# A second token quarter of the query projection in seven-product form, and reciprocals broadcast by one transfer per half quarter, in a fused attention and token-mixing kernel

## Chip, cores and metric

The kernel runs on one core of one Trainium2 chip. The metric is the device time of one execution in microseconds (us). TensorE (PE) does the matrix products and loads its stationary operand as separate instructions (PEld); VectorE (DVE), ScalarE (ACT) and GpSimd (POOL) work beside it; SyncE (SP) issues nearly all transfers, which run on 16 DMA engines.

## What is computed

x has 2048 tokens (S) of 1024 numbers (D), in bf16. A linear-attention block with 32 heads of 32 is followed by an MLP that mixes tokens (F = 3584). The part that matters here is the attention:

```python
qkv = (layernorm(x) @ wqkv).reshape(B, S, 3, H, Dh).transpose(2, 0, 3, 1, 4)
q, k, v = qkv[0], qkv[1], qkv[2]
phi = lambda t: where(t > 0, t + 1, exp(t)) + 1e-6
pq, pk = phi(q), phi(k)
kv = einsum("bhsd,bhse->bhde", pk, v)
z = einsum("bhsd->bhd", pk)
num = einsum("bhqd,bhde->bhqe", pq, kv)
den = einsum("bhqd,bhd->bhq", pq, z)[..., None] + 1e-6
h = x + (num / den).transpose(0, 2, 1, 3).reshape(B, S, D) @ wo
```

Behind it stands `h + B(layernorm(h))` with `gelu(u @ w1 + b1) @ w2 + b2` over tokens; the change does not touch it.

## The kernel before, in words

**Tiling.** The token axis is cut into four quarters u = 0 to 3 of 512 tokens (`SW`, `NSC`), the features into eight blocks j of 128. `xnT` holds the normalised x transposed, `pqT` holds phi(q) transposed, [128, 8, 2048].

**Key and value steps.** `run_step` (L1119) writes out by hand the order of a pipeline of steps, `KRun` (keys) and `VRun` (values), each on 256 tokens with number q. A step is a Strassen-like scheme of seven products p1 to p7 in place of eight, each of four 128x512 matmuls (`Run.mm`, L973). It needs sums of token blocks (`x_sums`, L962, kept in `xs_sb`) and of weight blocks (`w_sums`, L947). `kv_accum` (L923) adds phi(k)ᵀv into `kv_ps`.

**The query projection in two forms.** One quarter, u = 2, is done in seven-product form by two steps of class `QRun` (one for each half of the features), between the steps of q = 5; a `QRun` product is eight matmuls of 256 columns (L1107). Its four weight sums are `tq`, two of which lie in `shared_sb`, two in the part of `pqT` of quarter 3. The other three quarters are done in plain form, in 24 units (u, j) of eight matmuls of 512 columns, listed in `q_units` (L1312). Units 0 to 7 (u = 0) are issued early by `q_fill` (L1302): three beside the first value step, and five around and behind the last value step. Units 8 to 23 (u = 1 and 3) come in a later loop, `for n, (u, j) in enumerate(q_units[8:])`, as `q_held`. Every unit ends in `phi_evac`: ACT makes an Exp and a Relu tile (L185, L187), DVE makes phi from them (L190, L194).

**What else the later loop does.** Tables say behind which n each of these follows. `fold` (four times) multiplies the kv blocks into wo (16 small matmuls, two copies on ACT, two on DVE). `den(u)` makes the denominators of a quarter (8 matmuls) and their reciprocals by Ln and Exp on ACT, and writes them, 128x512 fp16, to `rd_dram`. `den_spread(u)` reads them back so that each of the 32 rows of a head gets its head's reciprocal: for each half h of the features four transfers of 32 partitions x 4 x 512, 128 KB each, into one of three buffers (`thirds`). `scale_q(u, h)` multiplies that half of `pqT` by them on DVE. `first_sums` prepares the next stage on DVE (`sa`, `is`).

**The output stage.** `out_mm(i)` for 16 token tiles, 16 matmuls each (8 blocks j for each of two output halves), reads the scaled `pqT` of its quarter, in the order of `place(i)`; `seed(i)` copies x into its accumulators first (ACT), from rows that `load_xr` brought.

Accumulators come from `acc_tile`, which takes buffers of two pools in the order of `acc_ring`. What is marked `pin` or goes through `hv`, `ht`, `hs`, `hd` keeps the order in which it is written on its engine; the rest is put in place by the framework's scheduler. SP's transfers are issued in order: a transfer that waits holds up all behind it.

Of the kernel before, what the change touches and what calls it, by code (L numbers as in the profile page):

```python
# [21 lines left out]
DH = 32  # L22
# [8 lines left out]
def kernel(  # L31
# [13 lines left out]
    x = A_x.flatten_outer_dims()  # L45
# [3 lines left out]
    NS, ND, NF = S // P, D // P, F // P  # L49
# [5 lines left out]
    SW = min(BANK, S)  # L55
    NSC = S // SW
# [3 lines left out]
    QR = P // 4  # L60
# [8 lines left out]

    def more_acc(bufs):  # L70
        pool = accx.enter_context(tc.tile_pool(name="accx", bufs=bufs, space=PSUM))
        acc_ring[:] = [acc, pool, acc, pool, pool] if bufs == 3 else [pool, pool, pool, acc, acc, pool]

    def less_acc():
        accx.close()
# [703 lines left out]
    with ExitStack() as actx:  # L779
# [27 lines left out]
            return (q + b) % HB  # L807

        with ExitStack() as a1:
            a1w = a1.enter_context(tc.tile_pool(name="a1w", bufs=1))  # L810
            wkv = a1w.tile([P, ND, 2 * D], BF16)
            NVA, NPK = 4, 4
# [21 lines left out]
            e1pool = a1.enter_context(tc.tile_pool(name="e1pool", bufs=1))  # L834
            epool = a1.enter_context(tc.tile_pool(name="epool", bufs=2))
            xin = a1.enter_context(tc.tile_pool(name="xin", bufs=3))
            a1s = a1.enter_context(tc.tile_pool(name="a1s", bufs=4))
            trctx = ExitStack()
# [113 lines left out]
                v = xnT[:, :, q * 2 * P:(q + 1) * 2 * P].rearrange("p (k two) (h f) -> p k two h f", two=2, h=2)  # L952
                return v[:, :, 0, 0, :], v[:, :, 1, 0, :], v[:, :, 0, 1, :], v[:, :, 1, 1, :]

            def x_sums(q, part=slice(0, 4)):
                a11, a12, a21, a22 = x_blocks(q)
                sm = xs_sb[:, q % 2]
                for out, a, b, op in (
                    (sm[:, 0], a21, a22, ALU.add), (sm[:, 1], sm[:, 0], a11, ALU.subtract),
                    (sm[:, 2], a11, a21, ALU.subtract), (sm[:, 3], a12, sm[:, 1], ALU.subtract),  # L960
                )[part]:
                    pin(nc.vector.tensor_tensor(out, a, b, op))  # L962

# [124 lines left out]
            class QRun(KRun):  # L1088
                lean = True

                def __init__(self, u, half):
# [3 lines left out]
                    self.s1, self.s2, self.s3, self.s4 = (  # L1095
                        xs_sb[:, :, t].rearrange("p r k f -> p k r f") for t in range(4)
                    )
                    (self.b11, _, self.b21, self.b22), (self.t1, self.t2, self.t3, self.t4) = qmov

# [16 lines left out]
                def dst(self, h, c):  # L1116
                    n0 = self.u * SW + h * SW // 2
                    v = pqT[:, 4 * self.half:4 * self.half + 4, n0:n0 + SW // 2]
                    return v.rearrange("p (j two) n -> p j two n", two=2)[:, :, c, :]  # L1119

            def run_step(n, prev, after6=None, after5=None, after7=None, fill=None, after3=None):
                if n is not None:
# [186 lines left out]
                phi_evac(pqT[:, j, u * SW:(u + 1) * SW], qp[:, 0:SW], SW, a2k)  # L1309

            assert NSC == 4
            q_units = [(u, j) for u in (0, 1, NSC - 1) for j in range(ND)]  # L1312
            NVP = NS // 2
            q_next = iter(q_units)

            def q_fill():
                q_unit(*next(q_next))
# [20 lines left out]
            load_next(2 * G0)  # L1338
            prev = v1
            q_sums = {2: slice(0, 1), 3: slice(1, 2), 4: slice(2, 3), 5: slice(3, 4)}  # L1340
            for q in range(2, NVP):
                runs = [KRun(q), VRun(q)]
                if q == 5:
                    runs = [runs[0], QRun(q // 2, 0), runs[1], QRun(q // 2, 1)]
                for n in runs:
                    kind = type(n).__name__[0]
                    i = {"K": 2 * q + 3, "V": 2 * q + 4}.get(kind, NS)
                    if q == 5 and kind == "Q":
                        i = NS - 1 if n.half == 1 else NS
                    elif q == 6 and kind == "K":  # L1350
                        i = NS

                    def after6():
                        if i < NS:
                            ln_stats(i)

                    def after5():
                        if kind == "V":
                            kv_accum(2 * q - 2)
                            kv_accum(2 * q - 1)  # L1360
                        if i < NS:
# [24 lines left out]
            nc.vector.memset(zz[:, :, 3 * HB:], float(S))  # L1386
            turned = kvbd[:].rearrange("p (b a) (r e) -> p a b r e", b=HB, e=DH)
            sums_v = kv_ps[:, :, 0:DH].rearrange("p (b a) e -> p a b e", b=HB)
            for q in range(HB):
# [25 lines left out]
        pools["is_bufs"] = 4  # L1415
        a3p = actx.enter_context(ExitStack())
        ndp = a3p.enter_context(tc.tile_pool(name="ndp", bufs=2, space=PSUM))
        rd_dram = [dram.tile([P, SW], FP16, name=f"rd_dram{u}") for u in range(NSC)]

        with ExitStack() as a3:  # L1420

# [44 lines left out]
            def den_inv(u, ps):  # L1466
                hs.activation(ps[:], ps[:], ACT.Ln, bias=eps_den[:], scale=1.0 / S)
                hs.activation(rd_sb, ps[:], ACT.Exp, scale=-1.0)
                hd.dma_start(rd_dram[u][:], rd_sb)

            def den_spread(u):
                rows = rd_dram[u].rearrange("(g o h) n -> o h g n", g=4, h=HB)
                for h in range(2):
                    rdb = thirds[(2 * SPREAD.index(u) + h) % 3].bitcast(FP16).rearrange("p (j n) -> p j n", n=SW)
                    for q in range(HB):
                        hd.dma_start(
                            rdb[q * DH:(q + 1) * DH, :, :],
                            rows[h, q].unsqueeze(0).to_broadcast([DH, 4, SW]),
                        )
                    rdbs[u, h] = rdb  # L1480

            def den(u):
                den_inv(u, den_mm(u))
# [98 lines left out]
            for n, (u, j) in enumerate(q_units[8:]):  # L1582
                if n == len(q_units) - 8 - 1:
# [8 lines left out]
                if n == 3:  # L1592
                    for i in range(XRL + 1):
                        load_xr(i)
                if n in (12, 13):
                    load_w1(1, n % 2, pin)
# [259 lines left out]
```

## Time and profile before

| | |
|---|---|
| median of 3 runs | 555.93 us (555.36 to 556.04) |
| the profiled execution, its own time | 556.6 us |
| its span, first to last instruction | 554.8 us |
| TensorE busy, share of the span | 548.8 us, 99% |
| VectorE, ScalarE, GpSimd busy | 444.6, 289.0, 26.3 us |
| mean granted TensorE clock | 0.999 of full speed |
| bytes moved by the 16 DMA engines | 74.58 MB, mean 134 GB/s |

Times in the profile are counted from the first instruction of the span. The 1.8 us between the span and the profiled execution's own time lie around the span. A row of the timeline gives the start, the length, the engine, the line and the operation, its output and inputs, and in brackets how long the engine had been idle before it, and who ended that. The chain of waits is followed back from the last instruction; a piece names the engine, the output tile, the line and the number of instructions. Through the helpers `ht`, `hs`, `hv` and `hd` many operations share line 230.

The change lies between 107 us (the key step of q = 6) and 190 us (the first tiles of the output stage). In this stretch the list of waits names none of a matmul. VectorE is busy 6.68 us of the ten from 110, 5.53 of the ten from 120, 7.68 of the ten from 150, 9.38 of the ten from 160 and 7.34 of the ten from 170.

### The profile page before, as it was taken

The numbers are of one execution on the slowest core, as the hardware profiler recorded it, in microseconds if no ns is written. First come the engines' busy times: TensorE is split into PE (matmuls) and PEld (weight loads), VectorE is DVE, ScalarE is ACT, GpSimd is POOL, SyncE is SP. The second block draws the span as 40 slices with busy tenths as digits, with TensorE's granted clock in tenths as the row PEclk, the third lists the DMA queues.
The fourth block names the chain that finished last, engine by engine and source line by source line (L and its number), as shares of the span: only waits on it lengthen the run. The fifth ranks groups of instructions, "written<-read, shape, count | busy, mean of one in ns | idle before, by whom it ended". The sixth has DMA issues, their size and how long they took to land.

```text
span 554.8 us, 9799 instructions
## 1 busy us (share of the span) xinstructions
PE 548.8 (99%) x3801; PEld 316.3 (57%) x3819; DVE 444.6 (80%) x863; ACT 289.0 (52%) x614; POOL 26.3 (5%) x36
## 2 busy tenths in 40 slices
PE   9999999999999999999999999999999999999997
PEld 3444446644444444456666766666445667667665
DVE  6798888764597788889989789888986979749747
ACT  4747768675886877645546465564210412413310
POOL 1000000000000000000000000000002103103111
PEclk9999999999999999999999999999999999999999
DMA  8933331204677942103041340423868759849334
GB/s 296 311 77 77 77 78 39 40 1 141 207 205 224 314 167 78 71 1 123 30 152 29 125 152 2 152 48 86 220 219 207 201 138 241 211 143 219 91 108 74
DMA packets 83087, 74.58 MB, mean 134 GB/s; under 512 B 15826, under 2 KB 74464, under 8 KB 83040
## 3 DMA queue, kind: packets, MB, share of 16 engines
q1 hardware_dynamic: 78656, 69.87, 42.4%
q0 software_dynamic: 4096, 3.68, 4.9%
q8 instruction: 30, 0.49, 0.4%
q10 hardware_dynamic: 288, 0.39, 0.2%
q14 instruction: 17, 0.14, 0.1%
HBM read 59.12 MB, written 11.67 MB: 128 GB/s over the span
## 4 chain that ended last, share of the span: by engine, by line
PE 98%; issue 0%; ACT 0%; DVE 0%; DVEq 0%
PE psI L230 25%; PE psC L230 16%; PE acc_t L230 15%; PE psB L230 8%; PE psC L973 4%; PE psB L973 4%; PE psA L973 4%; PE acc_t L893 4%; PE acc_t L1302 2%; PE psB L342 2%; PE psA L342 2%; PE psE L973 2%; PE psC L342 2%; PE psA L230 1%; PE psE L342 1%; PE acc_t L97 1%
## 5 line engine op out<-in xcount | busy, mean ns | idle before, releaser
L230 PEld LDWEIGHTS <-is 128*128 128x128 f16 x736 | 71.8, 98 | 31.1 <-DVE hi L230 0.4
L230 PEld LDWEIGHTS <-sa 128*128 128x128 f16 x606 | 59.2, 98 | 27.1
L230 PEld LDWEIGHTS <-wq 128*128 128x128 bf16 (+1 forms) x496 | 48.5, 98 | 28.1 <-issue 1.0
L230 PE MATMUL acc_t<-wo_sb,pqT 128*128 128x512 f16 x256 | 55.6, 379 | 0.0
L487 POOL DMA_DIRECT2D out_dram<-wq x28 | 24.4, 935 | 516.5 <-DVE sa L334 397.5
L230 PEld LDWEIGHTS <-pqT 128*128 128x128 bf16 x256 | 25.0, 98 | 30.5 <-issue 0.6
L230 DVE TENSOR_TENSOR t<-psI,t 128x256 f32<-128x256 f32 (+1 forms) x45 | 20.8, 475 | 22.2 <-PE psI L230 20.9
L230 PE MATMUL psC<-gs,wq 128*128 128x512 f16 x140 | 34.1, 379 | 0.0
L973 PEld LDWEIGHTS <-xs 128*128 128x128 f16 x208 | 19.7, 98 | 22.4 <-DVE xs L962 0.8
L190 DVE TENSOR_SCALAR e_sb<-e_sb 128x512 bf16<-128x512 bf16 x64 | 18.5, 289 | 17.1 <-ACT e_sb L185 16.8
L230 PE MATMUL psC<-hT,sa 128*128 128x512 f16 x112 | 31.2, 379 | 0.0
L230 PE MATMUL psI<-hi,is 128*128 128x256 f16 x200 | 30.0, 273 | 0.0
L230 PE MATMUL psB<-hT,sa 128*128 128x512 f16 x112 | 29.7, 379 | 0.0
L230 PE MATMUL acc_t<-xnT,wq_sb 128*128 128x512 bf16 x124 | 28.8, 380 | 0.2
L230 DVE BATCH_NORM_STATS2 hst<-acc_t 128x6 f32<-128x512 f32 x32 | 21.4, 692 | 8.9 <-ACT h_bf L230 8.9
L185 ACT ACTIVATE e_sb<-acc_t 128x512 bf16<-128x512 f32 x32 | 19.1, 597 | 17.3 <-PE acc_t L1302 9.5
L973 PE MATMUL psA<-wkv,xnT 128*128 128x512 bf16 x96 | 25.9, 379 | 0.4
L973 PEld LDWEIGHTS <-xnT 128*128 128x128 bf16 x156 | 15.2, 97 | 18.7 <-issue 1.1
L230 ACT CAST h_bf<-acc_t 128x512 bf16<-128x512 f32 x32 | 18.4, 583 | 12.4 <-PE acc_t L230 12.4
L230 PE MATMUL psC<-hT,wq 128*128 128x512 f16 x96 | 24.6, 379 | 0.0
L230 DVE TENSOR_TENSOR e<-psI,es 128x256 f32<-128x256 f32 x20 | 8.5, 425 | 19.9 <-PE psI L230 19.9
L230 ACT COPY psI<-psI 128x256 f32<-128x256 f32 x50 | 18.0, 360 | 11.6 <-PE psI L230 9.7
(245 smaller groups left out, 1123.0 us busy)
## 6 DMA issues: line engine op xcount, KB each, us to landing
wq<-in_B_w_dram SPq DMA_DIRECT2D x14, 1024.0 KB, 7.7
gs<-parked SPq DMA_DIRECT2D x9, 896.0 KB, 4.6
wq<-in_B_w_dram SPq DMA_DIRECT2D x6, 896.0 KB, 8.7
wq<-in_B_w_dram SPq DMA_DIRECT2D x12, 448.0 KB, 7.0
shared_sb<-rd_dram SPq DMA_DIRECT2D x32, 128.0 KB, 3.9
out_dram<-h_bf SPq DMA_DIRECT2D x16, 256.0 KB, 2.0
x_sb<-in_A_x_dram SPq DMA_DIRECT2D x14, 256.0 KB, 3.0
w2o<-in_B_w_dram SPq DMA_DIRECT2D x4, 896.0 KB, 10.2
```

The source lines that it names most:

```text
L97: pin(nc.tensor.matmul(ps[0:lhsT.shape[-1], 0:rhs.shape[-1]], lhsT=lhsT, rhs=rhs, start=True, stop=True))
L185: pin(nc.scalar.activation(e_sb[:], src, ACT.Exp))
L190: pin(nc.vector.tensor_scalar(e_sb[:], e_sb[:], 1.0, PHI_EPS, ALU.min, ALU.add))
L230: return (lambda *a, **kw: pin(op(*a, **kw))) if self.always or getattr(Held, self.key) else op
L342: pe.matmul(ps[:, cols], lhsT=lhs[:, k, :], rhs=mv(k)[:, cols], start=(start and k == 0), stop=(k == self.nk - 1), skip_group_check=True,)
L487: nc.gpsimd.dma_start(to, ot[:, a:b], accum_op=ALU.add)
L893: mm = nc.tensor.matmul(pp[:, 0:CW], lhsT=xnT[:, kt, i * P:(i + 1) * P], rhs=wkv[:, kt, c * CW:(c + 1) * CW], start=(kt == 0), stop=(kt == ...
L973: pin(nc.tensor.matmul(ps[:], lhsT=lhs[:, k, :], rhs=rhs[:, k, :], start=(start and k == 0), stop=(k == hk2 - 1), skip_group_check=True,))
L1302: nc.tensor.matmul(qp[:, 0:SW], lhsT=wq_sb[:, kt, j * P:(j + 1) * P], rhs=xnT[:, kt, u * SW:(u + 1) * SW], start=(kt == 0), stop=(kt == ND ...
```

## The change

Quarter u = 1 is taken out of the plain units and done by two more `QRun` steps behind the last value step, so that 16 plain units are left: five early ones, and eleven in the later loop (three of u = 0, eight of u = 3). The token sums for the two new steps are written over `xnT` of quarter 2, which has no reader left by then, beside the last key and value steps. `kv_accum` of the last two tiles moves into the second of the two. The pools of the fp32 sums are opened ahead of the others so that these stay alive longer. The reciprocals are laid out in `rd_dram` with the four rows of a head side by side, and a half quarter is spread by one transfer of 128 partitions x 2048 where it was four of 32 x 4 x 512. Order and tables of the later loop are rewritten: quarter 1 comes first, then 0, then 2; the scaling of quarter 2 moves into the output stage. `place` takes the permuted token order of a `QRun` for u = 1 as well.

```diff
-        acc_ring[:] = ... else [pool, pool, pool, acc, acc, pool]
+        acc_ring[:] = ... else [pool, pool, pool, pool, acc, acc]
...
-            def x_sums(q, part=slice(0, 4)):
+            def x_sums(q, part=slice(0, 4), home=None):
                 a11, a12, a21, a22 = x_blocks(q)
-                sm = xs_sb[:, q % 2]
+                s1, s2, s3, s4 = [xs_sb[:, q % 2, t] for t in range(4)] if home is None else home[q % 2]
...
+            def sums_home(u):
+                v = xnT[:, :, u * SW:(u + 1) * SW].bitcast(FP16)
+                parts = [[v[:, 4 * r + t, :].rearrange("p (k f) -> p k f", f=P) for t in range(4)] for r in range(2)]
+                both = v.rearrange("p (r t) (k f) -> p t k r f", r=2, f=P)
+                return parts, [both[:, t] for t in range(4)]
...
-            q_units = [(u, j) for u in (0, 1, NSC - 1) for j in range(ND)]
+            q_units = [(u, j) for u in (0, NSC - 1) for j in range(ND)]
...
+            late_parts, late_home = sums_home(2)
+            late_sums = {("K", 6): ((2, slice(0, 2)),), ("K", 7): ((2, slice(2, 4)), (3, slice(0, 1))), ("V", 7): ((3, slice(1, 4)),)}
...
+                        for x in late_sums.get((kind, q), ()):
+                            x_sums(x[0], x[1], late_parts)
...
-            run_step(None, prev, fill=q_fill)
-            q_fill()
-            kv_accum(NS - 2)
-            kv_accum(NS - 1)
-            for n in range(3):
-                q_fill()
+            r1, r2 = (QRun(1, half, late_home) for half in range(2))
...
+            run_step(r1, prev)
+            run_step(r2, r1, after6=last_accum)
+            run_step(None, r2, fill=q_fill)
+            q_fill()
...
-        rd_dram = [dram.tile([P, SW], FP16, name=f"rd_dram{u}") for u in range(NSC)]
+        rd_dram = [dram.tile([QR, 4, SW], FP16, name=f"rd_dram{u}") for u in range(NSC)]
...
-            SPREAD = (0, 2, 1, 3)
+            SPREAD = (1, 0, 2, 3)
...
-                hd.dma_start(rd_dram[u][:], rd_sb)
+                hd.dma_start(rd_dram[u].rearrange("r g n -> g r n"), rd_sb)
...
             def den_spread(u):
-                rows = rd_dram[u].rearrange("(g o h) n -> o h g n", g=4, h=HB)
                 for h in range(2):
-                    rdb = thirds[(2 * SPREAD.index(u) + h) % 3].bitcast(FP16).rearrange("p (j n) -> p j n", n=SW)
-                    for q in range(HB):
-                        hd.dma_start(
-                            rdb[q * DH:(q + 1) * DH, :, :],
-                            rows[h, q].unsqueeze(0).to_broadcast([DH, 4, SW]),
-                        )
-                    rdbs[u, h] = rdb
+                    rdb = thirds[(2 * SPREAD.index(u) + h) % 3].bitcast(FP16)
+                    rows = rd_dram[u][h * HB:(h + 1) * HB].rearrange("q g n -> q (g n)")
+                    hd.dma_start(rdb, rows.unsqueeze(1).to_broadcast([HB, DH, 4 * SW]))
+                    rdbs[u, h] = rdb.rearrange("p (j n) -> p j n", n=SW)
...
-                return i if u != 2 else NSC * u + r % 2 * 2 + r // 2
+                return i if u not in (1, 2) else NSC * u + r % 2 * 2 + r // 2
...
-            sums_at, ahead = (4, 8, 9, 11, 13), first_sums()
-            scale_at = {5: (0, 0), 6: (0, 1), 10: (2, 0), 12: (2, 1), 15: (1, 0)}
-            den_at = {0: 0, 2: 2, 9: 1}
-            spread_at = {0: 0, 6: 2, 12: 1}
+            sums_at = (0, 1, 2, 4, 6)
+            den_at = {0:1,3:0,8:2}
+            spread_at = {0:1,4:0,9:2}
+            scale_at = {3:(1,0),5:(1,1),7:(0,0),8:(0,1)}
...
-            scale_at = {0: (1, 1), 6: (3, 0), 8: (3, 1)}
+            scale_at = {1: (2, 0), 2: (2, 1), 6: (3, 0), 8: (3, 1)}
```

In the later loop `load_xr` of the first four rows moves from n = 3 to n = 2, and the two `load_w1` of the next weights from n = 12 and 13 to n = 7 and 8.

More of the change, by code (lines that the diff above doesn't have):

```diff
@@ L71, in more_acc @@
         pool = accx.enter_context(tc.tile_pool(name="accx", bufs=bufs, space=PSUM))
-        acc_ring[:] = [acc, pool, acc, pool, pool] if bufs == 3 else [pool, pool, pool, acc, acc, pool]
+        acc_ring[:] = [acc, pool, acc, pool, pool] if bufs == 3 else [pool, pool, pool, pool, acc, acc]
     def less_acc():
@@ L809 @@
         with ExitStack() as a1:
+            e1pool = a1.enter_context(tc.tile_pool(name="e1pool", bufs=1))
+            epool = a1.enter_context(tc.tile_pool(name="epool", bufs=2))
             a1w = a1.enter_context(tc.tile_pool(name="a1w", bufs=1))
@@ L833 @@
             spool = a1.enter_context(tc.tile_pool(name="spool", bufs=1))
-            e1pool = a1.enter_context(tc.tile_pool(name="e1pool", bufs=1))
-            epool = a1.enter_context(tc.tile_pool(name="epool", bufs=2))
             xin = a1.enter_context(tc.tile_pool(name="xin", bufs=3))
@@ L953, in x_blocks @@
                 return v[:, :, 0, 0, :], v[:, :, 1, 0, :], v[:, :, 0, 1, :], v[:, :, 1, 1, :]
-            def x_sums(q, part=slice(0, 4)):
+            def x_sums(q, part=slice(0, 4), home=None):
                 a11, a12, a21, a22 = x_blocks(q)
-                sm = xs_sb[:, q % 2]
+                s1, s2, s3, s4 = [xs_sb[:, q % 2, t] for t in range(4)] if home is None else home[q % 2]
                 for out, a, b, op in (
-                    (sm[:, 0], a21, a22, ALU.add), (sm[:, 1], sm[:, 0], a11, ALU.subtract),
-                    (sm[:, 2], a11, a21, ALU.subtract), (sm[:, 3], a12, sm[:, 1], ALU.subtract),
+                    (s1, a21, a22, ALU.add), (s2, s1, a11, ALU.subtract),
+                    (s3, a11, a21, ALU.subtract), (s4, a12, s2, ALU.subtract),
                 )[part]:
@@ L1089, with __init__ @@
                 lean = True
-                def __init__(self, u, half):
+                def __init__(self, u, half, home=None):
                     self.u, self.half, self.phi = u, half, {}
@@ L1095, in __init__ @@
                     self.s1, self.s2, self.s3, self.s4 = (
-                        xs_sb[:, :, t].rearrange("p r k f -> p k r f") for t in range(4)
+                        xs_sb[:, :, t].rearrange("p r k f -> p k r f") if home is None else home[t] for t in range(4)
                     )
@@ L1378, with last_accum @@
                     prev = n
-            run_step(None, prev, fill=q_fill)
-            q_fill()
-            kv_accum(NS - 2)
-            kv_accum(NS - 1)
-            for n in range(3):
-                q_fill()
+            r1, r2 = (QRun(1, half, late_home) for half in range(2))
             nc.vector.memset(zz[:, :, 0:3 * HB], 0.0)
             nc.vector.memset(zz[:, :, 3 * HB:], float(S))
+            def last_accum():
+                kv_accum(NS - 2)
+                kv_accum(NS - 1)
+            run_step(r1, prev)
+            run_step(r2, r1, after6=last_accum)
+            run_step(None, r2, fill=q_fill)
+            q_fill()
             turned = kvbd[:].rearrange("p (b a) (r e) -> p a b r e", b=HB, e=DH)
@@ L1574, in first_sums @@
                 yield cur
-            sums_at, ahead = (4, 8, 9, 11, 13), first_sums()
-            scale_at = {5: (0, 0), 6: (0, 1), 10: (2, 0), 12: (2, 1), 15: (1, 0)}
-            den_at = {0: 0, 2: 2, 9: 1}
+            ahead = first_sums()
+            sums_at = (0, 1, 2, 4, 6)
             fold_at = {1: 0, 3: 1, 5: 2, 7: 3}
-            spread_at = {0: 0, 6: 2, 12: 1}
+            den_at = {0:1,3:0,8:2}
+            spread_at = {0:1,4:0,9:2}
+            scale_at = {3:(1,0),5:(1,1),7:(0,0),8:(0,1)}
             kv_transpose()
-            for n, (u, j) in enumerate(q_units[8:]):
-                if n == len(q_units) - 8 - 1:
+            late_units = list(q_next)
+            for n, (u, j) in enumerate(late_units):
+                if n == len(late_units) - 1:
                     seed(0)
@@ L1591 @@
                     den_spread(spread_at[n])
-                if n == 3:
+                if n == 2:
                     for i in range(XRL + 1):
                         load_xr(i)
-                if n in (12, 13):
-                    load_w1(1, n % 2, pin)
+                if n in (7, 8):
+                    load_w1(1, (n + 1) % 2, pin)
                 if n in scale_at:
```

## The prediction

> **What bounds the kernel now.** I read the page's busy times first, then the chain of waits.
>
> ```profile
> PE 548.8 (99%) x3801; PEld 316.3 (57%) x3819; DVE 444.6 (80%) x863; ACT 289.0 (52%) x614; POOL 26.3 (5%) x36
> ...
> PE 98%; issue 0%; ACT 0%; DVE 0%; DVEq 0%
> ```
>
> The reader is to see that TensorE is the path: 98% of the chain is matmuls that follow each other, so a matmul taken out gives its whole length, as long as no new wait comes. The same chain, opened between 86 and 180 us, prices the two forms of a query projection:
>
> ```profile
> 89.73 0.87 PE psB L1107 x8
> ...
> 135.12 1.73 PE acc_t L1302 x8
> ...
> 142.73 2.17 PE acc_t L230 x16
> ...
> 170.17 8.03 PE acc_t L230 x36
> ```
>
> A seven-product piece (8 matmuls of 256 columns) takes 0.87 us, a plain unit 1.73; the transposes of kv cost 2.17 - 1.73 = 0.44. The last line ends at 178.20 with the 16 matmuls of the first output tile (3.46 us), which so began at 174.74.
>
> **Part 1, TensorE.** Eight plain units go: 8 x 1.73 = 13.84 us. Two steps of seven products come: 14 x 0.87 = 12.18 us. Taken alone that is **-1.66 us**. Folds, denominators, `kv_accum` and transposes keep their number.
>
> **Part 2, what is hidden.** Eight token sums (0.42 us each, as the rows of L962) go to VectorE beside the steps of q = 6 and 7, where it is busy 6.68 and 5.53 us of ten; the last stand some 0.9 us ahead of the product that reads them. Without that cover they would cost up to 3.4 us. In the two new steps I followed each accumulator from its matmul through ScalarE's copy (0.57), Exp and Relu (1.1) to its next writer, by the same rows at 88 to 98 us: no product waits, the closest has 0.5 us to spare. The weights w1 are loaded behind the moved `kv_accum`, 4.4 us later (142 in place of 137.58); the transfers of that load keep the engines busy for 8.6 us now, so it lands at 150.6, and VectorE wants it at 153. The ring of accumulators and the memsets move at no cost that a row shows.
>
> **Part 3, VectorE's queue in the later loop.** Behind the last value step (its final product ends at 131.67) TensorE has 14 x 0.87 + 2 x 0.86 + 0.59 + 2 x 1.73 = 17.95 us of work up to the transposes, which so start at 149.65; with 0.44, a unit, a denominator (0.6) and a unit, unit n = 1 ends at 154.17. VectorE's copies of the first fold then start at 155.73 (Exp and Relu behind the unit, as now). From there VectorE is never idle. What one thing costs it, start to start:
>
> ```profile
> 160.49 1.22 DVE L230 TENSOR_TENSOR pqT<-pqT,shared_sb 128x2048 bf16<-128x2048 bf16 x1
> 161.62 0.29 DVE L190 TENSOR_SCALAR e_sb<-e_sb 128x512 bf16<-128x512 bf16 x1
> 162.02 0.43 DVE L194 TENSOR_TENSOR pqT<-e_sb,r_sb 128x512 bf16<-128x512 bf16 x1
> 162.36 1.28 DVE L230 CAST wo_sb<-acc_t 128x512 f16<-128x512 f32 x2
> 163.56 0.28 DVE L190 TENSOR_SCALAR e_sb<-e_sb 128x512 bf16<-128x512 bf16 x1
> ...
> 173.64 0.42 DVE L230 TENSOR_TENSOR is<-sa 128x512 f16<-128x512 f16 x1
> ...
> 175.10 0.29 DVE L190 TENSOR_SCALAR e_sb<-e_sb 128x512 bf16<-128x512 bf16 x1
> ```
>
> So a scaling costs 1.13, a unit's pair 0.74, the two copies of a fold 1.20, the four `is` sums 1.46; an `sa` sum 1.14 (164.29 to 165.43). In the changed program VectorE's queue holds, from that fold to the scaling of (0, 1): 4 folds, 3 `sa`, 7 pairs, 4 scalings, `is` = 4.80 + 3.42 + 5.18 + 4.52 + 1.46 = 19.38 us; the last one's own length adds 0.09: it ends at 175.2. Added up in order, VectorE comes to scaling (1, 0) at 161.9, (1, 1) at 166.8, (0, 0) at 172.1, (0, 1) at 174.0. The first output tile reads blocks 4 to 7 of quarter 0 as its fifth matmul: 174.74 + 0.86 = 175.60 now, 173.94 by TensorE alone after the change, 175.2 by VectorE. So even with all transfers in time some 1.3 of the 1.66 us go back, and **-0.4 us** is left. The reason is that the loop lost five units of TensorE's work and kept VectorE's folds and sums and four of its five scalings.
>
> **Part 4, the broadcast transfers.** Scalings wait for them, and everything behind on VectorE waits with them: units' pairs, copies of folds (whose accumulators TensorE needs), and the first output tile.
>
> ```profile
> q1 hardware_dynamic: 78656, 69.87, 42.4%
> ...
> 196.00:198.00 2.00, 2.00 (x11) 0.93 (x10) 1.20 (x3) 1.82 (x5) 0.00 (x0) 1.00 1.05 390
> ...
> shared_sb<-rd_dram SPq DMA_DIRECT2D x24, 128.0 KB, 3.8
> ...
> wo_sb<-in_A_wo_dram SPq DMA_DIRECT2D x1, 512.0 KB, 3.9
> ...
> 147.24 0.35 SPq L230 DMA_DIRECT2D rd_dram<-shared_sb  x1
> 149.20 3.95 SPq L230 DMA_DIRECT2D shared_sb<-rd_dram  x8
> ```
>
> The lines are the page's queue, two microseconds at the highest rate, the transfers by size, and SP's own rows. Now SP takes 3.95 us to issue eight pieces; two issues take about 1, so 3 us per quarter leave SP's queue, where nothing waited for them. What a half of 512 KB takes in the new shape no row shows. Fast end: the 512 KB of wo, 3.9 us. Slow end: a transfer can be dealt out to DMA engines only in pieces that its pattern lists. Every large transfer in this trace lists 32, 64, 96 or 128 outer rows, all multiples of 16. The new pattern lists four outer rows of 32 copies each, and so does the write to `rd_dram` (4 x 32). If an outer row goes to one engine, four engines carry all of it. One engine moves 390 / 16 = 24.4 GB/s at best, and 69.87 MB in 42.4% of 16 x 554.8 us, 18.6 GB/s, on average. A half then takes 131 KB / 24.4 = 5.4 us (7.0 at 18.6) beside a fixed 1.6 (the write's 1.96 us from 147.24 to 149.20, less 0.34 for its bytes), and halves, x rows and weights line up behind each other on those four. I take the slow end at 24.4: by its outer count the new shape is nearest to a single 128 KB piece per outer row, and packets of 4 KB are longer than the mean of 888 bytes behind the 18.6.
>
> The Trainium skill has a rule for this ("DMA: Bandwidth & Descriptors", "Why a DMA increments its semaphore by 16 and not by 1"): a transfer runs on the largest number of engines, at most 16, that divides the outermost count of both sides. No run here shows it yet; by it 4 and 128 give four engines and the slow end, and the sum would be the one below, without it the -0.4 us of part 3.
>
> Slow end, step by step. The reciprocals of quarter 1 are ready at 154.2 (Ln and Exp behind the denominators at 152.4); written by 154.2 + 1.6 + 1.34 = 157.2; half (1, 0) lands at 164.2, (1, 1) at 169.6. The four x rows, issued behind them, put 65.5 KB on each of those engines: 2.7, to 172.3. The write for quarter 0, ready at 161.6, lands at 173.6; (0, 0) lands at 173.6 + 7.0 = 180.6, (0, 1) at 186.0. SP issues the latter only once scaling (1, 0) has freed its buffer, which is long past; behind it stand w1 and the write of quarter 2. The scaling ends at 187.2, the fifth matmul of the first output tile starts at 187.3: **+11.7 us**. Then on the same four engines: half of w1 2.7, write 1.34, other half 2.7, two halves of quarter 2, 10.8, and the x row of tile 4, 0.67: 204.2. Its seed takes 0.6: tile 4 starts at 204.8. By TensorE it could start at 187.3 + 2.6 (rest of tile 0) + 0.6 (denominators) + 3 x 3.46 = 200.9; before it starts at 189.1 (178.74 + 3 x 3.46). **Sum: 204.8 - 189.1 = +15.7 us.** Behind that all later transfers are in time, and TensorE bounds again.
>
> Against its own execution that is a span of 554.8 + 15.7 = 570.5, and 572.3 with the 1.8 us around it; the median of the runs lies 0.7 below the profiled execution, so 555.93 + 15.7 = **571.6 us**.
>
> TensorE would stand idle twice for over 5 us there. The granted clock is 1.00 in every stretch now, where it never does. The skill ("TensorE: Matmul & The Clock Gate", "Part 1") says that after a window of 3.4 us idle the clock halves until a busy one; no run here shows that; it would add an estimated 1 to 3 us, most of it hidden under the wait for tile 4's x row.
>
> **Rivals.**
> - *Transfers in time* (not slower). The halves spread over 16 engines and land in about 3.9 us: (1, 0) at 154.2 + 1.96 + 3.9 = 160.1, wanted at 161.9; (0, 0) at 167.5, wanted at 172.1. It decides as long as each lands ahead of VectorE. For it: each half is as many bytes as the wo row, with longer pieces. Then VectorE's queue sets the start of the output stage: 555.93 - 0.4 = 555.5 us, no change that counts.
> - *Full gain.* Transfers in time and VectorE at least 1.3 us quicker than my sum, so TensorE alone counts: 554.3 us. Against it: the costs come from a stretch in which VectorE ran without a gap.
> - *Slower engines in the slow case.* At 18.6 GB/s the same steps give out-tile 4 at about 218.6, +29.5 us; the far end, which longer packets speak against.
>
> **Chances.** Four-engine transfers 0.74, with 571.6; in time and VectorE-bound 0.16; full gain 0.10. Within 0.2% (1.1 us, about what a measurement of this kernel can tell from no change) lies the second: faster 0.10, same 0.16, slower 0.74. The range starts at 555.3, which takes in the second case, since the slow case with its own spread (563 to 580, an engine between 30 and 21 GB/s) holds less than 8 in 10.
>
> **What would show it.** Right: time from issue to landing of 7 us and more for the 512 KB halves; VectorE idle ahead of scaling (1, 0) and for over 5 us ahead of (0, 0) and (0, 1); TensorE waiting at the first output tile and once more near tile 4. Part 1: 28 pieces of L1107 at 0.87 us, and transposes near 149.7. Wrong: landings near 4 us, and VectorE busy without a gap from 156 to 175.

## The result, and the profile after

The changed kernel takes **590.36 us** (median of 4 runs, 589.04 to 591.38) against 555.64 before: +34.7 us, ratio 1.0623 (95% interval 1.0600 to 1.0646). The forecast was 571.6, range 555.3 to 580.0. Its direction and its mechanism (transfers on four engines) were right; its size was not: +15.7 was forecast, and the time lies 10.4 us above the range.

The page's busy times and its chain of waits, as shown of the kernel before:

```profile
PE 556.2 (94%) x3867; PEld 322.2 (55%) x3867; DVE 450.6 (76%) x875; ACT 289.8 (49%) x616; POOL 26.3 (4%) x36
...
PE 84%; DMA 12%; ACT 1%; DVE 1%; issue 0%; SPq 0%; ACTq 0%; DVEq 0%
...
L230 DVE TENSOR_TENSOR pqT<-pqT,shared_sb 128x2048 bf16<-128x2048 bf16 x8 | 9.7, 1214 | 24.1 <-DMA shared_sb<-rd_dram 24.1
```

TensorE fell from 98% to 84% of the chain and transfers took 12%, where they had none. The last row is the scalings: VectorE stood idle ahead of them for 24.1 us, all of it for the halves. The chain between 156 and 234 us names the transfers:

```profile
156.57 10.37 DMA shared_sb<-rd_dram
...
177.93 18.57 DMA rd_dram<-shared_sb
...
197.74 15.14 DMA xr<-in_A_x_dram
...
218.90 14.65 DMA out_dram<-h_bf
```

A half of 512 KB, then the 128 KB write of quarter 2's reciprocals, the x row of output tile 4, and an output tile's write. The issues of the halves of quarters 1 and 0, and the scalings (1, 0), (0, 0) and (0, 1) that waited for them:

```profile
156.57 1.12 SPq L230 DMA_DIRECT2D shared_sb<-rd_dram  x2
175.82 1.12 SPq L230 DMA_DIRECT2D shared_sb<-rd_dram  x2
...
166.96 1.23 DVE L230 TENSOR_TENSOR pqT<-pqT,shared_sb 128x2048 bf16<-128x2048 bf16 x1 [6.10 <-DMA shared_sb<-rd_dram]
187.02 1.23 DVE L230 TENSOR_TENSOR pqT<-pqT,shared_sb 128x2048 bf16<-128x2048 bf16 x1 [9.76 <-DMA shared_sb<-rd_dram]
192.48 1.22 DVE L230 TENSOR_TENSOR pqT<-pqT,shared_sb 128x2048 bf16<-128x2048 bf16 x1 [3.50 <-DMA shared_sb<-rd_dram]
```

So the first half of quarter 1 took 10.4 us from its issue to its scaling, that of quarter 0 11.2. TensorE's own rows in the output stage (in brackets: how long it had been idle, and who ended that) are:

```profile
188.30 1.89 PE L230 MATMUL acc_t<-wo_sb,pqT 128*128 128x512 f16 x4 [8.60 <-DVE pqT L230]
193.76 5.20 PE L230 MATMUL acc_t<-wo_sb,pqT 128*128 128x512 f16 x12 [3.57 <-DVE pqT L230]
...
213.54 16.75 PE L230 MATMUL acc_t<-wo_sb,pqT 128*128 128x512 f16 x64 [3.57 <-DVE pqT L230]
235.69 29.74 PE L230 MATMUL acc_t<-wo_sb,pqT 128*128 128x512 f16 x128 [5.40 <-ACT acc_t L230]
```

The rows are tile 0 (its first four matmuls, then the fifth), tile 4 and tile 8. Ahead of tiles 4 and 8 ScalarE's seeds set the start. Tile 4 reads quarter 1, which had long been scaled; the scaling named in its brackets is one of quarter 2, which ended within 0.1 us of the first half of tile 4's seed (in e7 below, tile 4 started at 208.15, ahead of the end of that scaling at 208.27). ScalarE's rows (the seed of tile 4, and the copy that the seed of tile 8 stood behind) show what they waited for:

```profile
212.90 1.11 ACT L230 CAST acc_t<-xr 128x512 f32<-128x512 bf16 x2 [5.34 <-DMA xr<-in_A_x_dram]
...
233.66 1.07 ACT L230 CAST h_bf<-acc_t 128x512 bf16<-128x512 f32 x2 [8.04 <-DMA out_dram<-h_bf]
```

To compare positions, count from a mark that both kernels pass: the `kv_accum` row at 117.25 before and at 116.07 after (the profiled execution of before had lost that 1.2 us in the first 40 us, which no change touches). The kernel before:

```profile
117.25 0.67 PE L923 MATMUL kvps<-vaug,pk 128*32 128x33 bf16 x64
...
174.58 3.61 PE L230 MATMUL acc_t<-wo_sb,pqT 128*128 128x512 f16 x16
178.13 0.61 PE L230 MATMUL den_ps<-pqT,zz 128*32 128x512 bf16 x8
178.68 51.97 PE L230 MATMUL acc_t<-wo_sb,pqT 128*128 128x512 f16 x240
230.49 3.62 PE L230 MATMUL psA<-hE,wq 128*128 128x512 f16 x16
```

A matmul there takes 0.216 us, so the fifth stands at 175.44, tile 4 at 189.1 and tile 8 at 202.9. Behind the mark the fifth matmul is 19.5 us later in the changed kernel (193.76 - 116.07 = 77.69, against 58.19), tile 4 25.7 later, tile 8 34.0, and the next stage's first product (`psA` from `hE`: 265.3, before 230.5) 36.0. The profiled executions differ by 36.0 - 1.2 = 34.8. So all of it arises between the first scaling and the end of the output stage.

A window of two microseconds and one of four, of the changed kernel (the last three columns are TensorE's granted clock, the mean busy share of the 16 DMA engines, and GB/s):

```profile
166.00:168.00 2.00, 0.03 (x1) 0.00 (x0) 1.04 (x1) 0.83 (x2) 0.00 (x0) 1.00 0.26 102
168.00:172.00 4.00, 0.00 (x0) 0.00 (x0) 3.79 (x9) 0.00 (x0) 0.00 (x0) 0.50 0.25 101
```

While only the halves run (behind 170 the last x packets too), a quarter of the engines is busy, at 101 GB/s: four engines at 25 GB/s. That is the claim of part 4. TensorE meanwhile waits, and its clock is halved.

### The profile page after: what moved, and what is told of

Read it like the earlier page. It is cut to its first block, busy times and chain, and to the rows that moved or that the text cites. A ratio compares the mean times of both kernels' runs of the same rounds, so it can differ in the third digit from the quotient of the medians.

```text
span 589.6 us, 9887 instructions
## 1 busy us (share of the span) xinstructions
PE 556.2 (94%) x3867; PEld 322.2 (55%) x3867; DVE 450.6 (76%) x875; ACT 289.8 (49%) x616; POOL 26.3 (4%) x36
## 4 chain that ended last, share of the span: by engine, by line
PE 84%; DMA 12%; ACT 1%; DVE 1%; issue 0%; SPq 0%; ACTq 0%; DVEq 0%
PE psI L230 24%; PE psC L230 15%; PE psB L230 8%; PE acc_t L230 6%; PE psC L973 4%; PE psB L973 4%; PE psA L973 4%; DMA rd_dram<-shared_sb 4%; DMA xr<-in_A_x_dram 4%; PE acc_t L893 3%; DMA out_dram<-h_bf 2%; PE psB L342 2%; PE psA L342 2%; PE psE L973 2%; DMA shared_sb<-rd_dram 2%; PE psC L342 2%
## 5 line engine op out<-in xcount | busy, mean ns | idle before, releaser
L230 PE MATMUL acc_t<-wo_sb,pqT 128*128 128x512 f16 x256 | 64.1, 417 | 21.2 <-DVE pqT L230 15.7
L230 PEld LDWEIGHTS <-pqT 128*128 128x128 bf16 x256 | 26.5, 105 | 58.3 <-issue 19.3
L487 POOL DMA_DIRECT2D out_dram<-wq x28 | 24.4, 935 | 551.2 <-DVE sa L334 432.3
L230 DVE TENSOR_TENSOR pqT<-pqT,shared_sb 128x2048 bf16<-128x2048 bf16 x8 | 9.7, 1214 | 24.1 <-DMA shared_sb<-rd_dram 24.1
L230 PE MATMUL psI<-gi,is 128*128 128x256 f16 x168 | 22.3, 273 | 0.0
```

Source lines behind the costliest of these rows:

```text
L230: return (lambda *a, **kw: pin(op(*a, **kw))) if self.always or getattr(Held, self.key) else op
L487: nc.gpsimd.dma_start(to, ot[:, a:b], accum_op=ALU.add)
```

## The experiments

The time of the kernel before beside them was 555.26 to 555.48 us. Positions are those of each run's own profile.

### Undoing the listing: e1, e2, e3, e4, e8

**e1_old_spread**: the changed kernel with the spreading of before.

```diff
-                hd.dma_start(rd_dram[u].rearrange("r g n -> g r n"), rd_sb)
+                hd.dma_start(rd_dram[u][:], rd_sb)
...
-                    hd.dma_start(rdb, rows.unsqueeze(1).to_broadcast([HB, DH, 4 * SW]))
+                    for q in range(HB):
+                        hd.dma_start(
+                            rdb[q * DH:(q + 1) * DH, :, :],
+                            rows[h, q].unsqueeze(0).to_broadcast([DH, 4, SW]),
+                        )
```

> The changed kernel with the spreading of the reciprocals as before: the old layout of rd_dram, its plain write, four transfers of 32 x 4 x 512 per half. Theory FEW ENGINES (the listing with an outermost count of four puts the write and the halves on four DMA engines): all 34.7 us go and the time is 555.5 (VectorE sets the start of the output stage; fifth output matmul near 175.2), or 554.3 if TensorE alone counts. Rival LOOP ORDER (the new order of units, denominators, x rows and weights in the later loop costs the time, whatever the transfers are): above 570, with TensorE idle in the later loop.

Measured: 559.55 us, ratio 1.0081 (1.0065 to 1.0096). 30.8 of the 34.7 us go with the listing; 4 stay, which neither theory had.

**e2_rw32**: the new layout stays, only the listing changes.

```diff
-                    hd.dma_start(rdb, rows.unsqueeze(1).to_broadcast([HB, DH, 4 * SW]))
+                    for q in range(HB):
+                        hd.dma_start(rdb[q * DH:(q + 1) * DH, :], rows[q].unsqueeze(0).to_broadcast([DH, 4 * SW]))
...
-                hd.dma_start(rd_dram[u].rearrange("r g n -> g r n"), rd_sb)
+                for g in range(4):
+                    hd.dma_start(rd_dram[u][:, g, :], rd_sb[g * QR:(g + 1) * QR])
```

> The changed kernel with its new layout of rd_dram kept; only the listing is changed: each half as four transfers of 32 copies of 4 KB (outermost 32), the write as four transfers of 32 rows. FEW ENGINES: landings near 4 us, 555.5, as with the old spreading. Rival LONG PIECES (4 KB pieces that read the same row 32 times are slow by themselves, on any number of engines): landings of 7 us and more, above 570.

Measured: 558.06 us, 1.0057 (1.0034 to 1.0080). The transfers by size, from the stretch 140 to 200 us, have a landing of 3.2 us, and TensorE's rows show what is left:

```profile
shared_sb<-rd_dram SPq DMA_DIRECT2D x32, 128.0 KB, 3.2
```

```profile
175.21 2.76 PE L230 MATMUL acc_t<-wo_sb,pqT 128*128 128x512 f16 x12 [0.83 <-DVE pqT L230]
...
197.42 34.82 PE L230 MATMUL acc_t<-wo_sb,pqT 128*128 128x512 f16 x160 [1.53 <-ACT acc_t L230]
```

The same 4 KB pieces are quick on more engines, so LONG PIECES falls as the cause. The second row is a new wait, 1.5 us, at the seed of tile 6.

**e3_r8**: as e2, but each piece listed 8 x 4, and the write left as it is.

```diff
+                    for q in range(HB):
+                        hd.dma_start(rdb[q * DH:(q + 1) * DH, :], rows[q].unsqueeze(0).unsqueeze(0).to_broadcast([8, 4, 4 * SW]))
```

> The changed kernel with its write as it is (outermost 4), each half as four transfers of 8 x 4 copies of 4 KB: the same four pieces per half as in e2_rw32, but listed with an outermost count of 8. FEW ENGINES: while only these transfers run, the DMA engines' mean busy share is 0.50 at about 196 GB/s (0.25 at 98 GB/s in the changed kernel), a half takes 2.7 us of engine time in place of 5.4, and the time lies between 556 and 566. LONG PIECES: no better than the changed kernel by more than a few us, above 575.

Measured: 568.73 us, 1.0237 (1.0224 to 1.0251), 2.7 above the expected range and between the two ends. A window in which only halves run:

```profile
176.00:178.00 2.00, 0.00 (x0) 0.00 (x0) 1.05 (x1) 0.19 (x1) 0.00 (x0) 1.00 0.54 198
```

An outermost count of 8 gives half of the engines and 198 GB/s, where 4 gave 0.25 and 101. It is the count that sets the engines: the bytes, pieces and issues are those of e8.

**e4_before_one**: the kernel before with nothing but the new layout, write and spreading.

> The kernel before with nothing but the new layout, write and one transfer per half of the broadcast; units, order and tables stay as before. FEW ENGINES: the halves of quarter 1 land some 10 us later than before and hold VectorE ahead of the first output tiles' statistics; 562 to 585, about 570. LOOP ORDER: 555.9 within 1 us, since nothing of the order is changed.

Measured: 583.56 us, 1.0510 (1.0494 to 1.0525). Without any reordering the one-transfer spreading alone costs 28 us, near the top of the expected range and well above the 570 named as likely. LOOP ORDER falls as the main cause.

**e8_r32**: halves listed by 32 as in e2, the write still one transfer of 4 x 32.

> The changed kernel with only the halves listed by 32 (four transfers each); the write to rd_dram stays one transfer with an outermost count of four. It prices the write alone: FEW ENGINES on 128 KB costs 1.34 us of engine time in place of 0.34, but one issue in place of four (some 1.3 us of SP's queue); within 1.5 us of e2_rw32, 557 to 559.5.

Measured: 560.64 us, 1.0112 (1.0091 to 1.0132): 2.6 above e2, more than the 1.5 expected. In its profile the seed of tile 6 waits 3.1 us where e2 had 1.5, and the 160 matmuls behind it take 36.3 where e2 had 34.8. (The profiled execution of e8 was itself 1.6 us above the median of its runs.) Even a 128 KB write on four engines is not small.

### Why the forecast was short: e7, e11, e12, e15

**e7_after_w1late**: the changed kernel, with the weights moved.

```diff
-                if n in (7, 8):
-                    load_w1(1, (n + 1) % 2, pin)
...
+                if i in (4, 6):
+                    load_w1(1, i // 2 - 2, pin)
```

> The changed kernel (transfers on four engines) with only the two loads of the next weights moved behind the rows of output tiles 4 and 6. Theory SHARED ENGINES (a later transfer takes its turns beside an earlier one on the same engines, so the weights, issued behind the halves of quarter 0, still delayed them): half (0, 0) lands about 7 us after its issue in place of 11.2, (0, 1) 5.4 later, fifth output matmul near 189 in place of 193.8, time 580 to 586. Rival FIRST IN, FIRST OUT (as the prediction had it): (0, 0) lands as late as before the move, 11 us behind its issue; time within 2 us of 590.4.

Measured: 587.90 us, 1.0582 (1.0560 to 1.0600). Half (0, 0), issued at 174.6, let its scaling start at 184.4: 9.8 us, where the changed kernel has 11.2 (175.8 to 187.0). Neither theory fits, and the time lies between their ranges. The single packets in the trace tell more. Each kind of transfer has its own packet size: 4 KB the halves, 2 KB the x rows and the output tiles, 1 KB the weights and the writes to `rd_dram`. For the changed kernel, worked out from the trace's packet records:

```
us          KB moved as 4 KB  2 KB  1 KB   mean ns of a 4 KB packet
162 - 164              143    322     0    244
166 - 168              205      0     0    168
168 - 170              205      0     0    161
170 - 172               66    133     0    161
172 - 174                0    129    65     -
182 - 184              106      0   260    343
186 - 188              201      0     0    164
```

Two things are to be seen. First, on the four engines the order is first in, first out: the last x packets (2 KB, 86 ns each there; 262 KB, a quarter of the four rows) come only when the halves are through, and the write (1 KB) behind them. So SHARED ENGINES falls. Second, a 4 KB packet takes 161 ns while nothing else runs, and mostly more while x rows or weights come in beside it: 193 to 343 ns in the mean of two microseconds from 158 to 166 and from 180 to 186. That these slow it is not shown. From 224 to 228 it took 161 again beside some 200 KB of 2 KB packets in two microseconds. And in e7, with the weights gone, the 4 KB packets of half (0, 0) took 207 to 244 ns from 176 to 182, with nothing else moving. What slows the packets stays open.

**e11_q3_32**: the changed kernel with quarter 3 alone listed as in e2 (an `if u == NSC - 1` around both).

> The changed kernel with only quarter 3's write and halves listed by 32; quarters 1, 0 and 2 stay on four engines. Theory TAIL (the prediction's step 'behind that all later transfers are in time' is what failed: two halves of quarter 3 stand for 10.7 us on four engines ahead of the output tiles' writes, whose late landing holds ScalarE's copies and so the seed of tile 8): the 5.4 us wait at tile 8 and the halved clock behind it go, 581 to 584. Rival (the backlog of quarter 2 alone still holds the writes): within 2 us of 590.

Measured: 581.07 us, 1.0451 (1.0427 to 1.0475), 9.3 below the changed kernel, as TAIL expected. TensorE's rows:

```profile
213.56 8.75 PE L230 MATMUL acc_t<-wo_sb,pqT 128*128 128x512 f16 x32 [4.22 <-ACT acc_t L230]
222.75 34.69 PE L230 MATMUL acc_t<-wo_sb,pqT 128*128 128x512 f16 x160 [0.44 <-ACT acc_t L230]
```

Tile 4 still starts late (213.56), but the 5.40 us ahead of tile 8 are gone. They came from the writes of output tiles, which stood behind quarter 3's two halves on the four engines (the 14.65 us in the chain above). The profiled executions of the two kernels differ by 8.0, as the positions behind tile 4 do; the rest of the 9.3 lies within the spread of the runs.

**e12_filler** and **e15_filler_short**: the changed kernel with matmuls added that keep TensorE busy while it waits; their output is not used. e12 has 18 more inside tile 0; e15 has 28, 20, 28 and 13.

```diff
+                    ht.matmul(junk[0][:], lhsT=wf[:, 0, 0:P], rhs=wf[:, 0, 0:SW], start=True, stop=True, skip_group_check=True)
...
+                if i in (0, 4, 8):
+                    filler({0: 36, 4: 24, 8: 34}[i])
```

> The changed kernel with matmuls added whose result nobody reads, so that TensorE is busy while it waits: 36 ahead of output tile 0, 18 behind its first four matmuls, 24 ahead of tile 4, 34 ahead of tile 8 (0.216 us each, some 85% of each wait). Theory CLOCK (the granted clock of 0.5 behind the waits adds time of its own: tiles 4 to 7 took 16.75 us in place of 13.82, tiles 8 to 15 29.74 in place of 27.65): the clock stays at 1.00 there, those stretches take 13.8 and 27.7, time 583 to 588. Rival (the lower clock is hidden under the next wait): 590 as the changed kernel.

> e12_filler with fewer idle matmuls (28, 13, 20 and 28 in place of 36, 18, 24 and 34), since those of e12 ended up to 1.3 us behind the scalings and 0.8 behind the seed of tile 8 and so delayed what they were to accompany. CLOCK: the granted clock stays near 1.00 from 180 on and the time lies 3 to 5 us below the changed kernel, 585.5 to 587.5. Rival: 589 and more, as e12; the lower clock was hidden under the next wait.

Measured: 588.78 us (1.0580 to 1.0629) and 590.43 (1.0605 to 1.0646). The filler does what it should to the clock, as the row behind tile 8 of e15 shows (27.79 for the 128 matmuls, where the changed kernel has 29.74):

```profile
236.62 27.79 PE L230 MATMUL acc_t<-wo_sb,pqT 128*128 128x512 f16 x128
```

But tile 8, whose seed again stands behind an output tile's write, then starts 0.6 us later behind the mark than in the changed kernel (236.62 - 116.37). In e12 tiles 4 to 7 ran at full clock too (7.07 us for each two), and tile 8 starts only 0.7 earlier (234.95 - 116.04); the 2.9 us saved there were mostly waited for again. The time moves by 1.6 us in e12 and not at all in e15, no more than the runs spread. CLOCK as a cost of several us is not confirmed. By the rows it is some 2 us, those behind tile 8, where no transfer is waited for any more.

### What is left without the listing: e5, e6, e9, e10, e13, e14

**e5_rw32_w1late** is e2 with the weights moved as in e7; **e6_is_late** is e5 with the `is` sums moved as well:

```diff
-            sums_at = (0, 1, 2, 4, 6)
+            sums_at = (0, 1, 2, 4, 9)
```

> e2_rw32 (all broadcasts and writes on 16 engines) with the two loads of the next weights moved out of the later loop, behind the rows of output tiles 4 and 6 (first wanted near 245). Theory RESIDUE IS TRAFFIC (what e2 still loses, 2.6 us, is the bunching of 2 MB of weights, 2 MB of x rows and the broadcasts of quarters 2 and 3 between 168 and 205, which delays the write of an output tile and so the seed of tile 6 by 1.5 us): 556.5, no wait at a seed, output stage ending 1.5 earlier. Rival (the residue is the loop's own order on VectorE and TensorE): 558.0 unchanged.

> e5_rw32_w1late with the four is sums on VectorE moved from n = 6 to n = 9, behind the last scaling that the first output tile waits for. Theory VECTORE BOUND (part 3 of the prediction: VectorE's queue sets the fifth output matmul at 175.2, TensorE alone could reach 173.94): 1.3 us below e5, fifth matmul near 173.9, some 555.2. Rival (TensorE or ScalarE sets it too): no difference from e5.

Measured: e5 556.40 us, 1.0020 (1.0011 to 1.0028): 1.7 below e2, and no seed waits any more, as expected. e6 557.17, 1.0035 (1.0022 to 1.0048): no gain; the rival's result. **e9_old_w1late** is e1 with the weights moved, **e10_old_w1late_is** adds the `is` move:

> e1_old_spread (old layout, one plain write, eight transfers of 32 x 4 x 512 a quarter) with the two loads of the next weights moved behind the rows of output tiles 4 and 6, as in e5. Theory TRAFFIC: the last transfer of half (0, 1), which landed at 176.3 with the weights beside it, lands before 174; the 4.2 us wait ahead of the fifth output matmul shrinks under 1; 555.0 to 555.8. Rival (the wait comes from the queue in which SP issues the eight pieces, weights or not): above 557.

> e9_old_w1late with the four is sums on VectorE behind the last scaling for the first output tile (n = 9 in place of 6). Theory VECTORE BOUND, once transfers are in time (the plain write lands 1.4 us after its issue in place of 3.0 for four small ones, so the halves come earlier than in e6): fifth output matmul within 0.3 us of where TensorE alone puts it, 0.5 to 1.3 us below e9, near 554.4 and faster than the kernel before. Rival (half (0, 1)'s transfer is last here as in e6): no gain over e9.

Measured: e9 556.27, 1.0014 (1.0005 to 1.0023), 3.3 below e1 but not as far as expected; e10 556.13, 1.0018 (1.0006 to 1.0031), no gain again. VectorE's rows in e10 show why:

```profile
171.39 1.23 DVE L230 TENSOR_TENSOR pqT<-pqT,shared_sb 128x2048 bf16<-128x2048 bf16 x1 [2.07 <-DMA shared_sb<-rd_dram]
...
173.91 1.23 DVE L230 TENSOR_TENSOR pqT<-pqT,shared_sb 128x2048 bf16<-128x2048 bf16 x1 [0.56 <-DMA shared_sb<-rd_dram]
```

The 1.5 us taken off VectorE became a wait of 2.07 and 0.56 for quarter 0's halves. SP could issue these only at 166.50, when their write (issued 161.41) had landed, and 1 MB of x rows stood ahead of that write:

```profile
158.68 2.64 SPq L230 DMA_DIRECT2D shared_sb<-in_A_x_dram  x4
161.41 0.41 SPq L230 DMA_DIRECT2D rd_dram<-shared_sb  x1
166.50 3.65 SPq L230 DMA_DIRECT2D shared_sb<-rd_dram  x8
```

**e13_xr_early** and **e14_xr_early_is** are e9 and e10 with these x rows issued ahead of the loop:

```diff
-                if n == 2:
-                    for i in range(XRL + 1):
-                        load_xr(i)
...
+            for i in range(XRL + 1):
+                load_xr(i)
             kv_transpose()
```

> e9_old_w1late with the first four x rows (1 MB) issued ahead of the later loop, where the queue is idle, in place of between quarter 1's halves and quarter 0's write. Theory ORDER OF TRANSFERS (in e9 and e10 the x rows stand on the engines ahead of quarter 0's write, which lands 4.7 us after its issue, so half (0, 1) is the last to come and hides VectorE's own bound): no wait of a scaling for a transfer; VectorE, without a gap from the first fold, sets the fifth output matmul some 26 us behind the transposes' start, near 174.1 where e9 had 175.03: 555.3. Rival (the issue of eight pieces by SP is last): unchanged from e9, 556.3.

> e13_xr_early with the four is sums behind the last scaling (n = 9). VECTORE BOUND: 1.0 to 1.5 us below e13, fifth output matmul near 172.8, where TensorE alone would put it; about 553.9, 1.5 below the kernel before: the gain of part 1. Rival (transfers are still last): as e13, within 0.3 us.

Measured: e13 **555.55** us, 0.9999 (0.9990 to 1.0008); e14 **554.18** us, 0.9978 (0.9968 to 0.9987), faster than both kernels. In e13 none of VectorE's four scalings shows idle time in brackets, and the fifth matmul waits for the last of them:

```profile
160.59 1.21 DVE L230 TENSOR_TENSOR pqT<-pqT,shared_sb 128x2048 bf16<-128x2048 bf16 x1
165.53 1.21 DVE L230 TENSOR_TENSOR pqT<-pqT,shared_sb 128x2048 bf16<-128x2048 bf16 x1
170.78 1.22 DVE L230 TENSOR_TENSOR pqT<-pqT,shared_sb 128x2048 bf16<-128x2048 bf16 x1
172.65 1.22 DVE L230 TENSOR_TENSOR pqT<-pqT,shared_sb 128x2048 bf16<-128x2048 bf16 x1
```

```profile
173.92 2.76 PE L230 MATMUL acc_t<-wo_sb,pqT 128*128 128x512 f16 x12 [0.83 <-DVE pqT L230]
```

In e14 the 16 matmuls of tile 0 are one row with no wait:

```profile
172.58 3.63 PE L230 MATMUL acc_t<-wo_sb,pqT 128*128 128x512 f16 x16
```

## Why the prediction was right, and where it was wrong

**Part 1 (-1.66 us of TensorE).** Shown in part, once no transfer is late: e14 is 0.22% faster than the kernel before (0.13 to 0.32%), 1.2 us (0.7 to 1.8). By position its output stage starts 0.90 earlier (172.58 - 116.15 = 56.43, before 57.33). The other 0.76 are short pauses of TensorE in the later loop, which the forecast did not have: the 16 matmuls of the last fold take 0.77 where others take 0.43, with a wait of 0.17 behind them, and a denominator's 8 take 0.85 where others take 0.61.

**Part 2 (hidden work).** No product of the two new steps waits in the changed kernel's list, and the transposes start where the sum had them: they stand at 148.44, 32.4 behind the mark, and the forecast of 149.65 came to 32.4. The step held.

**Part 3 (VectorE takes 1.3 of the 1.66 back).** Shown by e13 and e14 as a pair. The forecast had the four scalings at 161.9, 166.8, 172.1 and 174.0; less the 1.37 by which the mark of e13 stands earlier these are 160.5, 165.4, 170.7 and 172.6, and e13 has 160.59, 165.53, 170.78 and 172.65. Counted from the mark, the fifth matmul of e13 stands at 173.92 - 115.88 = 58.0, of the kernel before at 58.2, and the forecast of 175.2 came to 57.9. With four sums moved behind the last scaling it stands 0.75 earlier (57.3) and the time falls by 1.4. But as long as the x rows stood ahead of quarter 0's write (e6, e10), the sums were not what came last: the same edit gave nothing there.

**Part 4 (four engines).** The mechanism is shown by e3 and e2: counts of 4 and 8 give shares of 0.25 and 0.54, and listing by 32 (e2) takes 32.3 us away; e3 and e8, which differ in the count of the halves alone (8 and 32), lie 8.1 us apart. The Trainium skill's rule ("DMA: Bandwidth & Descriptors", "Why a DMA increments its semaphore by 16 and not by 1"), the largest number of engines up to 16 that divides both outermost counts, agrees with both.

**What failed is the size, at two steps.** First, "I take the slow end at 24.4": the forecast gave each first half 7.0 us from issue to landing (5.4 at 24.4 GB/s and 1.6 fixed), and the rows show 10.4 for (1, 0) and 11.2 for (0, 0). Those 3.4 and 4.2 are nearly all of what the fifth matmul is late by: with the forecast shifted by the 1.2 us of the mark, it came 7.7 us late (193.8, forecast 186.1), and tile 4 9.9 late (213.5, forecast 203.6). Alone an engine does move 25 GB/s, but in these first halves a packet took up to twice as long. Why stays open: in the changed kernel x rows and weights came in beside them, but in e7 (0, 0) still took 9.8 us with nothing beside it.

Second, "behind that all later transfers are in time, and TensorE bounds again". They were not: behind tile 4 another 10.3 us came (36.0 - 25.7). 8.3 of them lie ahead of tile 8, whose seed stood behind an output tile's write: TensorE spent 2.9 of these on longer matmuls at half clock in tiles 4 to 7 (16.75, where 64 matmuls of 0.216 take 13.82) and 5.4 waiting. The other 2.1 are longer matmuls behind tile 8 (29.74, where 128 take 27.65). e11 takes 9.3 us away by changing quarter 3 alone. Together, less the 1.2 us that the profiled execution of before had lost by itself, 9.9 + 10.3 - 1.2 = 19.0 us, which is what the forecast lacked (34.8 - 15.7 = 19.1). I had followed the queue on the four engines up to the one transfer that I took for the last, and not to its end: quarter 3's halves and the output writes use the same four.

Of the signs that were named, one did not come: VectorE's idle time ahead of (0, 1) was 3.5 us and not over 5.

The rival "slower engines" (+29.5) came nearer to the time than the forecast, in part by luck. Its 18.6 GB/s is near what the two first halves got (237 and 278 ns in the mean for 4 KB, 17 and 15 GB/s), but it held this for every transfer on the four engines, while the second halves ran at 24 and 25, and it left out the tail behind tile 4 as well.

The clock, which the forecast put at 1 to 3 us, was halved in four stretches (their times stand below); that it cost more than some 2 us in all is not shown.

## What to carry to other kernels

Before several transfers are merged into one, look at the outermost count on both sides: one transfer of 4 x 32 rows ran on four engines, where four transfers of 32 rows kept up to 0.84 of the sixteen busy, and transfers of 8 x 4 about eight. When a transfer becomes slow, follow its queue until it is empty: each later transfer on the same engines is late too, also those that nobody waited for before. And an engine that bounds the start of a stage by 1.3 us shows itself only when the transfers that feed it are early: the same move of four sums gave nothing in e6 and e10 and 1.4 us in e14.

## What the runs showed of the hardware

- An issue on SP can itself be held up: with the weights' 1 MB ahead of it, the 128 KB write of quarter 2 kept SP for 10.44 us, and 0.54 when the weights were moved (e7).

```profile
177.93 10.44 SPq L230 DMA_DIRECT2D rd_dram<-shared_sb  x1
```

- The granted clock changes on a grid. In the changed kernel it fell near 168.0, 185.1, 212.4 and 232.9 and rose near 174.8, 198.7, 219.2 and 239.7; every distance is a multiple of 3.41 us (two, three or four of them). So TensorE, which stopped at 166.0 and at 179.7, lost its clock 2.0 us later the first time and 5.4 the second. The Trainium skill ("TensorE: Matmul & The Clock Gate", "Part 1") describes a window of 3.4 us that runs on by itself; these distances agree with it.
- 4 KB pieces that read one row 32 times did not reach the rate of other loads when they were listed by 32: in e2 they took 232 ns each in the median, and the windows 158 to 160 and 168 to 170 us, in which they run, show 211 and 268 GB/s at busy shares of 0.75 and 0.84, where the kernel before has 390 at 1.05. Why was not tried.
